# Attention products on four 64x64 TensorE tiles in a fused attention and feed-forward kernel

## The chip, the cores and the metric

One core of one Trainium2 chip. The metric is the device time of one execution in microseconds, the median of several runs. The profile is of one further execution, whose own time is given beside its span.

## What is computed

Eight batches of eight heads, 576 positions, head size 64, go through an attention whose softmaxes stand on the queries and keys alone, so that it is two small products per head. Its result, 4608 tokens of 512 features, goes through a two-layer network with a gated nonlinearity.

```python
q_s = softmax(q, axis=-1)                      # over the 64 features
k_s = softmax(k, axis=2)                       # over the 576 positions
kv  = einsum('bhsd,bhse->bhde', k_s, v)        # 64 x 64 per head
x   = einsum('bhsd,bhde->bhse', q_s, kv)       # then (batch, position) x (head, feature)
h   = x @ w_in                                 # 512 -> 2048
out = (h * sigmoid(beta * h)) @ w_out          # 2048 -> 512
```

## The kernel before

**Slabs.** The tokens are done in nine slabs of 512: slab t (0 to 7) is the first 512 positions of batch t, slab 8 the last 64 positions of all eight batches. Each slab has two halves of 64 full matmuls (128 rows, 128 columns, 512 moving columns, bf16). The first half (`pass1_tile`, L670; `pass1_mm`, L647) makes 16 tiles of 128 hidden features from four 128-feature parts of `XT`, rotating over the PSUM banks 0 to 2; ScalarE applies Silu with beta as scale (L655) into `GT`. The second half (`pass2_group`, L739) makes four groups u of 128 tokens over the 16 hidden tiles, in banks 3 and 4; VectorE copies the result out (L713) and SP stores it.

**Attention of one batch.** Heads are handled in four pairs hp. ScalarE takes exp of the queries (`exp_q`, L292) and keys (`exp_k`, L300). VectorE or GpSimd divides the queries by their sums (`norm_main`, L332) and a DMA transposes them into `QT` (`t_dma`, L454; batches 0 and 1 transpose on TensorE, `t_steps`, L376). The values are cast with a column of ones beside them (`cast_v`, L353). The keys' exps lie in `EK` as 128 columns per position group: for partitions 0 to 63 the first head's 64 features and zeros, for partitions 64 to 127 zeros and the second head's (a key tensor's partition holds nine consecutive positions of one head, 64 partitions per head). So one 128x128 matmul with 65 moving columns per group j (nine of them) accumulates the product of both heads of a pair and, in column 64, the keys' sums (`kv_steps`, L418). VectorE takes the reciprocal and scales the two 64x64 blocks into the diagonal of `KVD` (`kvd`, L403), whose other half is zero (`homes_vk`, L228). One 128x128 matmul per pair then gives the transposed output (`out_mm`, L438), which VectorE copies into `XT` (`out_step`, L443). The 64 remaining positions of two batches go together (`load_qrem`, L262; `exp_qr`, L327; `norm_rem`, L344; `tr_dma`, L462; `outr_steps`, L468), into `XT8` for slab 8. Batch 0's key-value product alone uses two 64x64 tiles (`kv_tiles`, L529), from keys' exps kept in `GT`.

**Order.** There are no queues of ready work: each engine runs its instructions in the order in which the program adds them, and `Program.plan` (L91) derives the semaphore waits from what each reads and writes. An instruction increments its engine's semaphore if any other one depends on it, also where only a later overwriting does. Matmuls of a slab are counted as slots 1 to 128 (`tick`, L785), 1 to 64 in the first half; a list `todo` gives the slot at which attention work is put between them. In slab t from 2 to 6 the attention of batch t+1 is done so (`attn`, L485): the 36 key-value matmuls one by one at slots 8 to 36, the four output matmuls at 84 to 108, for odd batches the remainder's eight at 104 to 120. Slab 1 does batch 2 (`attn_late`, L495, slots 103 to 124) and batch 1's remainder (101.5 to 103). In slab t ScalarE also takes the exps of batch t+2 after its Silus (L849 on): queries first, then the remainder's queries, then keys; then SP loads batch t+4.

**Loads.** SP issues one DMA each for a batch's queries, keys and values (`load`, L275), two for a pair of batches' remaining queries. Before the slabs stands a head (L604 to L643): weights are loaded and cast (`cast_win`, L579), batch 0's attention is done, and `warm` matmuls (L505) fill waits.

The softmax here doesn't subtract the row's maximum and nothing guards it: scores larger than these inputs give would overflow.

## Time and profile before

| what | value |
|---|---|
| time, median of 3 runs | 285.43 us (284.8 to 285.46) |
| the profiled execution's own time | 284.93 us |
| its span, first to last instruction | 283.1 us |
| TensorE matmuls busy | 277.9 us, 98%, 1608 matmuls |
| ScalarE busy | 177.6 us, 63% |
| VectorE busy | 117.0 us, 41% |
| GpSimd busy | 38.1 us, 13% |
| DMA, data queue of SP | 48.77 MB, 55.1% of the 16 engines' span |
| full matmuls of the two layers | 576 and 592 |
| key-value matmuls 128x128, 65 columns | 252 |
| output matmuls 128x128, 512 columns | 32 |

Matmuls are pipelined and the profile models their ends, so a matmul's mean duration (379 ns for 512 columns) is longer than the distance from one start to the next. What a matmul costs is read from starts: over a stretch, length by count. PE's busy share says that TensorE never lacks something to do, not that each thing is cheap. A line such as L373 is a helper through which all matmuls go, so groups are told apart by what they write and read. A bracket at a line's end is the idle time before it and what ended it.

### The profile page before, as it was taken

To read this page: it belongs to the slowest core of one execution; us is meant where nothing else is said; L and a number is where in the kernel's file an instruction comes from. 1 tells how busy PE (TensorE), PEld (TensorE's weight loads), DVE (VectorE), ACT (ScalarE), POOL (GpSimd) and SP (SyncE) were. 2 spreads that over 40 slices of the span, in tenths; PEclk is the share of its full clock that TensorE was granted. 3 is DMA by queue.
4 is the path that set the end of the run, shared out by engine and by line. 5 is a ranking of instruction groups with operands and counts; after the bars stand their busy time and mean duration, and the time that the engine had idled before them with its cause. 6 is when DMAs were issued, how large, how long until landed. Compare 5 with 4: busy or idle time off the path is not lost.

```text
span 283.1 us, 3950 instructions
## 1 busy us (share of the span) xinstructions
PE 277.9 (98%) x1608; PEld 136.3 (48%) x1608; DVE 117.0 (41%) x218; ACT 177.6 (63%) x243; POOL 38.1 (13%) x57
## 2 busy tenths in 40 slices
PE   7899999999999999999999999999999999999995
PEld 3545454445455445544554445444544444444443
DVE  4665786218781348124831473055705300110012
ACT  6767787989978926795579636892660076017500
POOL 6622041216121032100130000000000000000000
PEclk9999999999999999999999999999999999999999
DMA  7999999999998999217960033002700030012022
GB/s 249 371 390 400 391 371 307 361 341 248 330 329 248 358 360 296 39 34 251 374 104 1 2 148 74 2 1 98 141 4 0 9 141 0 0 54 96 0 74 74
DMA packets 41467, 50.07 MB, mean 177 GB/s; under 512 B 20325, under 2 KB 28773, under 8 KB 40297
## 3 DMA queue, kind: packets, MB, share of 16 engines
q1 hardware_dynamic: 40496, 48.77, 55.1%
q10 hardware_dynamic: 952, 1.06, 1.1%
q8 instruction: 12, 0.20, 0.3%
q14 instruction: 7, 0.05, 0.0%
HBM read 36.71 MB, written 9.44 MB: 163 GB/s over the span
## 4 chain that ended last, share of the span: by engine, by line
PE 98%; DVE 0%; ACT 0%; issue 0%
PE PS L373 97%; PE PS L371 1%; ACT XT L544 0%; DVE XT L219 0%; DVE KVD L411 0%; ACT VB L358 0%; DVE O2S L734 0%; DVE RC L520 0%
## 5 line engine op out<-in xcount | busy, mean ns | idle before, releaser
L655 ACT ACTIVATE GT<-PS,BETA 128x512 bf16<-128x512 f32 x144 | 96.7, 689 | 79.1 <-PE PS L373 79.1
L373 PE MATMUL PS<-WOUT,GT 128*128 128x512 bf16 (+2 forms) x592 | 132.8, 373 | 0.0
L373 PE MATMUL PS<-XT,WIN 128*128 128x512 bf16 x576 | 132.2, 379 | 0.0
L373 PEld LDWEIGHTS PS<-XT,WIN 128*128 128x128 bf16 x576 | 60.2, 106 | 59.2 <-ACT GT L655 0.4
L373 PEld LDWEIGHTS PS<-WOUT,GT 128*128 128x128 bf16 x592 | 55.4, 98 | 61.8
L713 DVE COPY O2S<-PS 128x512 f32<-128x512 f32 x33 | 22.7, 687 | 107.7 <-PE PS L373 107.7
L373 PE MATMUL PS<-VB,EK 128*128 128x65 bf16 x252 | 33.3, 193 | 0.0
L358 POOL CAST VB<-VF 128x576 bf16<-128x576 f32 (+1 forms) x29 | 21.1, 729 | 77.9 <-DMA VF<-in_v_dram 73.5
L309 ACT ACTIVATE EK<-KF 64x1152 bf16<-64x1152 f32 x24 | 27.8, 1157 | 0.4
L339 DVE TENSOR_REDUCE QS<-EQ 128x8 f32<-128x512 bf16 (+1 forms) x22 | 20.1, 913 | 15.4 <-ACT EQ L297 15.3
L373 PEld LDWEIGHTS PS<-VB,EK 128*128 128x128 bf16 x252 | 20.0, 98 | 6.5
L449 DVE CAST XT<-PS 128x512 bf16<-128x512 f32 x24 | 16.4, 690 | 10.9 <-PE PS L373 10.9
L297 ACT ACTIVATE EQ<-QF 128x512 bf16<-128x512 f32 x32 | 17.8, 619 | 2.0 <-DMA QF<-in_q_dram 1.8
L341 DVE TENSOR_TENSOR EQ<-EQ,QI 128x1024 bf16<-128x1024 bf16 (+1 forms) x14 | 15.9, 1132 | 0.5
L373 PE MATMUL PS<-QT,KVD 128*128 128x512 bf16 x32 | 12.2, 380 | 0.3 <-DVE KVD L411 0.3
L341 POOL TENSOR_TENSOR EQ<-EQ,QI 128x512 bf16<-128x512 bf16 x8 | 8.3, 1042 | 17.3 <-DVE QI L340 17.0
L373 PE MATMUL PS<-XT 128*128 128x512 f32 x10 | 7.7, 903 | 1.5 <-DVE XT L219 1.5
L411 DVE TENSOR_TENSOR KVD<-PS,RC 64x64 bf16<-64x64 f32 (+2 forms) x28 | 8.6, 308 | 0.9
L297 ACT ACT_TABLE_LOAD x6 | 7.7, 1283 | 0.1
L655 ACT ACT_TABLE_LOAD x5 | 6.4, 1283 | 0.1
L432 DVE RECIPROCAL RC<-PS 128x4 f32<-128x4 f32 (+2 forms) x9 | 1.6, 177 | 10.0 <-PE PS L373 9.9
L319 ACT ACTIVATE EK<-KF 64x576 bf16<-64x576 f32 (+1 forms) x6 | 5.0, 842 | 1.0 <-DMA KF<-in_k_dram 0.9
(54 smaller groups left out, 85.9 us busy)
## 6 DMA issues: line engine op xcount, KB each, us to landing
out_dram<-O2S SPq DMA_DIRECT2D x8, 1024.0 KB, 5.1
KF<-in_k_dram SPq DMA_DIRECT2D x6, 1152.0 KB, 8.4
VF<-in_v_dram SPq DMA_DIRECT2D x6, 1152.0 KB, 11.2
QF<-in_q_dram SPq DMA_DIRECT2D x6, 1024.0 KB, 7.6
KF<-in_k_dram SPq DMA_DIRECT2D x8, 288.0 KB, 8.3
VF<-in_v_dram SPq DMA_DIRECT2D x8, 288.0 KB, 8.6
WST<-in_moe_w_in_dram SPq DMA_DIRECT2D x8, 256.0 KB, 7.9
O2S<-in_moe_w_in_dram SPq DMA_DIRECT2D x4, 512.0 KB, 11.9
```

What stands on the lines that cost most here:

```text
L297: add(ACTE, lambda e, o=o, a=a: e.activation(o, a, ACT.Exp), r=[("qf", i, hp)], w=[("eq", i, hp)])
L309: add(ACTE, lambda e, o=o, a=a: e.activation(o, a, ACT.Exp), r=[("kf", i, h) for h in hps], w=[("ek", i, h, e_) for h in hps])
L319: add(ACTE, lambda e: e.activation(o, a, ACT.Exp), r=[("kf", i, h) for h in hps], w=[("ek", i, h, e_) for h in hps])
L339: add(DVE, lambda e: e.tensor_reduce(s_, a, AX.X, ALU.add), r=ks, w=[("qs", i, hp0)])
L341: add(eng, lambda e: e.tensor_tensor(a, a, vb, ALU.mult), r=ks + [("qi", i, hp0)], w=ks)
L358: add(eng, lambda e: (e.copy if eng == ACTE else e.tensor_copy)(o, a), r=[("vf", i, hp), ("vone", i)], w=[("vb", i, hp, h) for h in ((0, 1 ...
L371: add(PE, lambda e: e.transpose(o, l, r_), r=r, w=w, bank=[bk])
L373: add(PE, lambda e: e.matmul(o, l, r_, start=start, stop=stop, tile_position=tp), r=r, w=w, bank=[bk])
L411: add(DVE, lambda e, o=o, a=a, s_=s_: e.tensor_tensor(o, a, s_, ALU.mult), r=[("ps", bk)] + [("rc", i, h) for h in hps], w=[("kvd", i, h, ...
L449: add(eng, lambda e: (e.copy if eng == ACTE else e.tensor_copy)(XT[i][:, hp, :], PS[bk][:, :]), r=[("ps", bk)], w=[("xt", i, hp)], bank=[bk])
L655: add(ACTE, lambda e: e.activation(GT[:, f, :], PS[bk][:, :], ACT.Silu, scale=BETA[:, f:f + 1]), r=[("ps", bk), "beta"], w=[("gt", f)], ba ...
L713: add(eng, lambda e: (e.copy if eng == ACTE else e.tensor_copy)(O2S[t % 2][:, u, :], PS[bk][:, :]), r=[("ps", bk)], w=[("o2", t % 2, u)], ...
```

## The change

Batches 2 to 7 do both attention products on four 64x64 tiles of TensorE: tile (row, column) at (0,0), (64,64), (0,64), (64,0). The first two take the two heads of one pair, the other two those of the next pair, so that for pairs 1 and 3 the first head's product lands in the lower half of PSUM's partitions and the second's in the upper. For that the query load puts the heads of pairs 1 and 3 in swapped places, in four DMAs of two heads each in place of one (`load_swapped`), and the remainder's query load likewise in eight in place of two. Each output matmul swaps them back. `EK` now has 64 columns per group and no zeros for these batches, with one exp over all 128 partitions; `KVC` takes the place of `KVD` for them. `EKD`, with zeros, remains for batch 1.

All attention matmuls of a slab stand in one place: in slab t from 2 to 6 at slot 92, and the key-value product there is that of batch t+2, a slab earlier than before. In slab 1 the key-value product of batch 2 stands at slot 95 and a block at 113; the remainder of batch 1 at 94 to 95, on full matmuls as before. ScalarE takes the exps of the keys before those of the queries (batch 2 apart), and copies half of the outputs into `XT`.

```diff
+        SLOTS = ((0, 0, 1), (4, 4, 1), (2, 3, 4), (3, 2, 4))
+        def load_swapped(b):
+            i = b % 2
+            for x, (s0, d0, n) in enumerate(SLOTS):
+                a = bass.AP(qt_h, (b * H + s0) * S * D,
+                            [[4 * D, 128], [n * S * D, 2], [1, 4 * D]])
+                o = bass.AP(QF[i], d0 * 4 * D, [[H * 4 * D, 128], [n * 4 * D, 2], [1, 4 * D]])
+                add(SP, lambda e, o=o, a=a: e.dma_start(o, a),
...
+        def exp_kc(b, hp, n=1):
+            i = b % 2
+            o = bass.AP(EK[i], hp * KW, [[NHP * KW, 128], [1, n * KW]])
+            a = bass.AP(KF[i], hp * KW, [[NHP * KW, 128], [1, n * KW]])
...
+        def tile_mm(bk, ro, co, c, w, l, r_, start, stop, r):
+            mm(PS[bk][co:co + 64, c:c + w], l, r_, start, stop, r=r, w=[("ps", bk)], bk=bk,
+               tp=(ro, co))
+        def quad(hp):
+            return ((hp, 0, 0), (hp, 64, 64), (hp + 1, 0, 64), (hp + 1, 64, 0))
+        def kv_quads(b, bks):
+            i = b % 2
+            for a in (0, 2):
+                for j in range(NG):
+                    for hp, ro, co in quad(a):
+                        p = slice(ro, ro + 64)
+                        tile_mm(bks[hp % 2], ro, co, VW * (a // 2), D + 1, EK[i][p, hp, j, :],
+                                VB[i][p, hp, j, 0:D + 1], j == 0, j == NG - 1,
+                                [("ekc", i, hp), ("vb", i, hp, 0), ("vb", i, hp, 1), ("vone", i)])
+            for y in range(2):
...
+                add(DVE, lambda e, v_=v_, s_=s_: e.reciprocal(v_, s_), r=[("ps", bk)],
...
+                add(DVE, lambda e, o=o, p_=p_, vb=vb: e.tensor_tensor(o, p_, vb, ALU.mult),
...
+        def out_quads(b, bks):
+            i = b % 2
+            for a in (0, 2):
+                for hp, ro, co in quad(a):
+                    p = slice(ro, ro + 64)
+                    tile_mm(bks[hp], ro, co, 0, SM, KVC[i][p, hp, :], QT[i][p, hp, :], True, True,
+                            [("kvc", i, hp), ("qt", i, hp)])
             for hp in range(NHP):
+                eng, bk = (ACTE if hp % 2 else DVE), bks[hp]
...
+        def outr_quads(b, bks):
+            pi = b // 2
+            for a in (0, 2):
+                for e_ in range(2):
+                    for hp, ro, co in quad(a):
+                        p = slice(ro, ro + 64)
+                        tile_mm(bks[hp % 2], ro, co, 256 + (a // 2) * 128 + e_ * 64, 64,
+                                KVC[e_][p, hp, :], QTR[p, hp, 64 * e_:64 * e_ + 64], True, True,
+                                [("kvc", e_, hp), "qtr"])
...
+        def block(b):
+            out_quads(b, (5, 6, 7, 0))
+            if b % 2 and b > 1:
+                outr_quads(b, (1, 2))
+            if b + 1 < B:
+                kv_quads(b + 1, (1, 2))
...
-                todo = spread(outr_steps(1), 101.5, 103) + attn_late(2)
+                todo = spread(outr_steps(1), 94, 95)
+                todo += [(95, lambda: kv_quads(2, (1, 2))), (113, lambda: block(2))]
             elif t < 7:
-                todo = attn(t + 1)
+                todo = [(92, lambda: block(t + 1))]
```

The head is put in a new order. Batch 0's keys' exps lie in `EK[0]`; its last value cast is done whole by GpSimd (before, half by ScalarE), the cast of the weights' part 0, 3 by GpSimd in place of VectorE. Two long warm matmuls go and two short ones come; the second pair's transposes come before the first key-value product, the third output before the last product. The clearing of `EK[1]` in slab 0 goes.

```diff
         norm_main(0, 1, 1, POOL)
         go(t_steps(0, (0,), (3,)))
         turn_beta()
-        warm(1, 0, True)
         norm_main(0, 2, 1, POOL)
         norm_main(0, 3, 1, POOL)
+        go(t_steps(0, (1,), (4,)))
         kv_tiles(0, 7)
-        go(t_steps(0, (1,), (4,)))
-        warm(1, 0, True)
+        warm(1, 0)
         cast_v(0, 2)
-        cast_v(0, 3, POOL, 1)
-        cast_win(0, 1, POOL)
-        cast_win(0, 2, POOL)
+        cast_v(0, 3)
+        for m in range(1, NM):
+            cast_win(0, m, POOL)
         cast_win(1, 0, POOL)
         go(t_steps(0, (2,), (5,)))
+        warm(1, 0)
         kv_tiles(1, 1)
         out_now(0, 0, 0, ACTE)
         go(t_steps(0, (3,), (6,)))
         warm(1, 3)
+        kv_tiles(2, 7)
         out_now(0, 1, 5, ACTE)
-        kv_tiles(2, 7)
-        cast_v(0, 3, ACTE, 0)
         cast_win(0, 0, DVE)
         warm(1, 3)
+        out_now(0, 2, 0, ACTE)
         kv_tiles(3, 1)
-        out_now(0, 2, 0, ACTE)
```

## The prediction

> **What bounds the kernel now.** I read the page first. Its chain of work that ended last names one engine, and its slices show that engine full from the second slice on, while the DMA engines are full only for the first 16 slices (7.08 us each, so to about 113 us).

> ```profile
> PE   7899999999999999999999999999999999999995
> ...
> DMA  7999999999998999217960033002700030012022
> ...
> PE 98%; DVE 0%; ACT 0%; issue 0%
> ```

> So a TensorE nanosecond saved after some 113 us shortens the run; one saved earlier may only meet a transfer sooner. Next the busy time by stretch, one stretch per half slab (start and end, length, then busy time of PE, PEld, DVE, ACT, POOL). The slabs' starts come from the timeline of PE: slab 2 at 75.93, slab 7 at 224.69.

> ```profile
> 105.77:120.71 14.94, 14.94 (x102) 7.77 (x100) 7.03 (x10) 10.29 (x15) 3.30 (x4) 1.00 0.63 169
> 120.71:135.39 14.68, 14.68 (x70) 6.66 (x69) 4.74 (x7) 10.52 (x13) 0.00 (x0) 1.00 0.50 162
> 224.69:238.50 13.81, 13.81 (x66) 6.77 (x64) 0.69 (x1) 10.29 (x15) 0.00 (x0) 1.00 0.19 77
> 238.50:252.31 13.81, 13.81 (x65) 6.26 (x64) 2.08 (x3) 0.71 (x2) 0.00 (x0) 1.00 0.00 0
> ```

> Slab 7 has no attention: 13.81 us per half, 0.2158 us per matmul of 512 columns. Slab 3's first half, with 36 key-value matmuls, is 1.12 longer (31 ns each); its second, with four output matmuls, 0.86 longer (4 x 0.2158). Odd batches add 0.23 for eight remainder matmuls (14.91 in slabs 2, 4, 6). ACT is busy for 10.5 of 14.7 there, so it follows.

> Slabs 2 to 6 take 224.685 - 75.930 = 148.755; ten pure halves are 138.13. **The attention's whole price there is 10.62 us**; that is what can be won.

> **What the tiles cost in this trace.** The kernel already uses two tiles, in the head (batch 0). Timeline of PE (start, duration, line, count):

> ```profile
> 10.76 0.39 PE L371 MATMUL PS<-IDB,EQ 128*128 128x128 bf16 x4
> 11.08 0.47 PE L373 MATMUL PS<-VB,GT 64*64 64x65 bf16 x18
> 11.48 0.39 PE L373 MATMUL PS<-QT,KVD 128*128 128x512 bf16 x1
> ...
> 12.64 0.39 PE L373 MATMUL PS<-QT,KVD 128*128 128x512 bf16 x1 [0.33 <-DVE KVD L411]
> 12.96 0.47 PE L373 MATMUL PS<-VB,GT 64*64 64x65 bf16 x18
> 13.37 0.39 PE L373 MATMUL PS<-WARM 128*128 128x512 bf16 x1
> ```

> The 512-column matmul at 12.64 streams until 12.86; the next full one starts at 13.37. In between lie 0.51 us for 18 tile matmuls. Their single records show nine pairs, the second of a pair 3.5 ns after the first, pairs 32.4 ns apart: 0.29 us. The other **0.215 us is going into and out of the tiled mode** (0.10 and 0.11). A pair step of 32.4 ns equals the 31 to 32 ns of a full 65-column matmul[...].

> There is a second thing in the same place. VectorE waits for the last of those matmuls:

> ```profile
> 10.04 0.17 DVE L520 RECIPROCAL RC<-PS 128x1 f32<-128x1 f32 x1 [0.79 <-PE PS L371]
> ```

> The tile matmuls started between 9.205 and 9.489, yet the trace's semaphore records show PE's increments at 9.433, 9.467 and so on to 10.014: 34 ns apart. **Increments go one at a time, at 34 ns**, and the matmuls of a pair run ahead of them (16 ns each). At worst 15 were outstanding, and the stream did not slow.

> [...]

> **The change part by part.**

> *Key-value product, six batches.* Removed: 36 x 31.2 ns = 1.12 each. Added: 72 tile matmuls in 18 steps of four. At the pair's step this is 18 x 32.4 = 0.583. Bounds: 0.583 if four tiles go as fast as two; 1.17 if only two ever run together (36 steps); 2.45 (72 x 34 ns) if PE is held to the pace of its increments. I take 0.583: the pairs outran their increments, and a step didn't feel its instruction count.

> *Output, six batches.* 4 x 0.2158 = 0.863 becomes two steps of four, 0.432 (0.863 if in pairs). *Remainder, batches 3, 5, 7.* 0.234 becomes four steps, 0.130 (upper 0.54 by increments). *Mode changes.* One block costs 0.215; slab 1 has two.

> *Sum for slabs 2 to 6*, where a block holds output(t+1), the odd batch's remainder and key-value(t+2): slabs 2 and 4: 0.432 + 0.130 + 0.583 + 0.215 = 1.36; slabs 3 and 5: 1.23; slab 6 has no next batch: 0.78. Together 5.96 against 10.62: **4.66 us saved**, all on PE's chain.

> *Slab 1.* Before, its second half has 16.05 - 13.81 = 2.23 of attention. After: remainder of batch 1 unchanged 0.234, key-value(2) with its mode changes 0.80, then a block of 1.23: 2.26. No gain, and a new wait: the whole of output(2) now stands at slot 113, some 71.5 us, and the kernel goes no further until the transposed queries of pairs 2 and 3 are there. They are issued last behind batch 3's load:

> ```profile
> 66.01 3.76 SPq L459 DMA_TRANSPOSE QT<-EQ  x2
> ```

> They land at 70.48 and 71.69; before, pair 2 was wanted only at 73.3. From 71.69: 0.22 + 0.58 + 0.11 + 15 x 0.2158 = 4.15, so slab 2 can't start before 75.85 (75.93 now). Queued behind that wait on PE is everything; the DMA order that causes it is not changed, and the engines are full until there.

> *Head.* V's last cast goes from ScalarE (13.55 to 14.01) wholly to POOL, one weight cast from DVE to POOL, the transposes come before the product, two long warm matmuls go. The waits [0.40 <- ACT VB] and for the first weight cast shrink: landed at 13.09 it can be cast right after the third product's scaling, near 13.1 to 13.5, so the first layer starts near 13.65 in place of 14.99. The cover is thin: weights for columns 1024 on land at 20.39 and are wanted at 20.8, and in slab 0's second half batch 1's normalisation and the output weights are held by DMA. Timeline of DVE:

> ```profile
> 37.94 1.24 DVE L341 TENSOR_TENSOR EQ<-EQ,QI 128x512 bf16<-128x512 bf16 x1
> 39.10 2.08 DVE L569 TENSOR_SCALAR WOUT<-O2S,RB 128x512 bf16<-128x512 f32 x4
> ```

> The first of these scales is ready at 39.5; PE uses it at 40.28. So of 1.34 us at most 0.76 passes here, and the wait at 71.69 eats that. Head and slab 1 together: 0.0 to 0.8 saved, I take 0.1.

> *Covered work.* ScalarE: key exps go from four of 1157 ns to two (same columns, all partitions), 2.3 us less per slab; it takes two of the four XT copies (0.58 each) after its exps, which end about 7.3 us after a first half, where the copies come at 5.8; the next slab needs them only at 13.8. DVE: two copies of 0.69 less, four short scalings in place of three operations. POOL: casts unchanged; the second memset of slab 0 goes. SP: three more issues per query load, six more per remainder pair, at 0.43 to 0.5 us each, same packets; at most 4.5 us in a queue that otherwise waits for stores (111.9 us in the SP waits). Keys and values of batch 4 on are wanted 10 us earlier; the nearest, V(4), lands at 83.0 and is cast by 86.3, against some 96. All at nothing; if batch 3's cast (from 68.8) were late by 1 us, slab 1 pays 1 us.

> **The sum.** The profiled execution is 284.93, span 283.13 and 1.80 around it. 284.93 - 4.66 - 0.1 = 280.2; the same taken off the median 285.43 is 280.7. I say **280.5**.

> **Rivals.** (1) *Slower: the increments hold PE.* Nearly every tile matmul increments, because a later batch overwrites what it read. Batches 6 and 7 have no successor and escape. If few more than 15 can be outstanding, the products of batches 2 to 5 cost 2.45 each, 1.87 over; two fall into slab 1 (3.74, less 0.7 from the head), two into slabs 2 and 3 (3.74), the remainders of 3 and 5 add 0.41 each: -4.66 + 3.05 + 3.74 + 0.83 = +2.96, 288. It decides for slower above about 25 ns per tile matmul. For: 55 would be outstanding. Against: 15 left no mark. (2) *Only two tiles run at once*, so the change doesn't do what it says: +0.432 per output, +0.583 per product, +0.13 per remainder, 4.88 in slabs 2 to 6 and 1.6 - 0.7 in slab 1: +1.1, 286. For: the trace has only tiles that differ in rows and columns both. (3) *Only the products run at half pace*[...]: -4.66 + 2.72 + 0.47 = -1.5, 283.5. (4) *Head gain survives*: 279.6.

> **Chances.** Forecast 0.57, (1) 0.12, (2) 0.07, (3) 0.18, (4) 0.06. The range 279.2 to 285.5 takes in (3) and (4) and the bounds between; it leaves out (1) and (2), 0.19. About 0.3% (0.86 us) is what can be told from no change: faster means below 284.6. Forecast, (4) and most of (3) give 0.78 faster; 0.06 within; 0.16 slower.

> **What would show it.** Right: first halves of slabs 2 to 6 at 13.81, second halves near 15.1, slab 2's start near 75.9 with a short PE wait for the transposes before it; a product's 72 matmuls inside 0.6 us, VectorE's reciprocals some 2.5 us after the first of them. Wrong: tile matmuls 16 ns apart (rival 2 or 3) or 34 (rival 1), PE idle at slot 92 on key, value or query data, or the first layer not near 13.7.

## The result and the profile after

| what | before | after |
|---|---|---|
| time, median, side by side | 285.12 us (284.79 to 285.46) | 288.95 us (288.75 to 289.84) |
| ratio, 95% interval | | 1.014, 1.0114 to 1.0167 |
| the profiled execution's own time | 284.93 us | 288.75 us |
| its span | 283.13 us | 286.96 us |

The kernel is slower by 1.4%, where 280.5 was forecast. The page of after, its slices (7.17 us each), its chain of work that ended last, and the row of the tile matmuls of the key-value product:

```profile
PE   7899999999999799999999799999999999999995
...
DMA  7999999999999998607970006000640030002023
...
PE 75%; DMA 14%; SPq 5%; DVE 4%; issue 1%
...
L390 PE MATMUL PS<-VB,EK 64*64 64x65 bf16 x504 | 11.2, 191 | 3.3 <-DVE XT L556 3.0
```

Two slices of TensorE now stand at 7 that stood at 9: the 14th (93.3 to 100.4 us) and the 23rd (157.8 to 165.0). The chain is no longer TensorE from end to end. It runs back through VectorE, and through a DMA and SP's queue from there. The row names the releaser: VectorE's copy into `XT` at L556, the copy of the *remainder*. Next the half slabs of slabs 2 and 3, in the columns that the prediction used:

```profile
78.00:91.80 13.80, 13.75 (x65) 6.75 (x65) 7.66 (x10) 10.10 (x15) 3.01 (x4) 1.00 1.16 278
91.80:109.90 18.10, 16.29 (x160) 8.34 (x161) 4.76 (x11) 8.84 (x12) 2.68 (x4) 1.00 1.08 347
109.90:123.70 13.80, 13.75 (x64) 6.75 (x64) 6.29 (x7) 10.07 (x15) 4.21 (x4) 1.00 0.56 138
123.70:139.90 16.20, 15.99 (x144) 8.20 (x145) 4.10 (x9) 9.26 (x13) 0.00 (x0) 1.00 0.57 190
```

First halves are down to the 13.81 us of a half without attention. Second halves stand far above the forecast of 15.17 and 15.04, and the first of them has 1.8 us in which TensorE does nothing. Lengths of all halves, from one half's first weight load to the next one's (the after trace lacks 28 of 1168 full matmuls' own records, and has all of their weight loads; differences are taken before rounding):

| slab | before, whole slab | after, whole slab | difference | forecast |
|---|---|---|---|---|
| start of slab 1 | 44.91 | 44.41 | -0.50 | -0.1 with slab 1 |
| 1 | 14.76 + 16.05 | 14.76 + 18.79 | +2.75 | (row above) |
| 2 | 14.94 + 14.91 | 13.81 + 18.11 | +2.08 | -0.86 |
| 3 | 14.93 + 14.68 | 13.81 + 16.17 | +0.38 | -0.75 |
| 4 | 14.94 + 14.91 | 13.81 + 17.18 | +1.15 | -0.86 |
| 5 | 14.93 + 14.68 | 13.81 + 15.17 | -0.62 | -0.75 |
| 6 | 14.94 + 14.91 | 13.81 + 14.60 | -1.43 | -1.44 |

The differences make +3.80 of the span's +3.83. Slab 6, the one block without a product, came out as forecast; slab 5, whose product is batch 7's, nearly. Everything that failed lies in the products of batches 2 to 5, in the two blocks with a remainder ahead of a product, and in slab 1.

**A block with a remainder.** Timeline of TensorE in slab 2 (start, duration, line, operation, count, idle before):

```profile
98.13 0.63 PE L390 MATMUL PS<-QT,KVC 64*64 64x512 bf16 x8
98.59 0.29 PE L390 MATMUL PS<-QTR,KVC 64*64 64x64 bf16 x16
100.37 2.02 PE L390 MATMUL PS<-VB,EK 64*64 64x65 bf16 x72 [1.49 <-DVE XT L556]
102.55 1.24 PE L390 MATMUL PS<-WOUT,GT 128*128 128x512 bf16 x5 [0.16 <-issue]
```

The outputs take 0.46 from their start to the remainder's, as forecast (0.432). The remainder's 16 matmuls start within 0.10 us. Then TensorE waits, and the timeline of VectorE shows for what:

```profile
98.60 1.29 DVE L540 CAST XT<-PS 128x512 bf16<-128x512 f32 x2 [2.19 <-PE PS L390]
99.81 0.75 DVE L556 CAST XT<-PS 128x256 bf16<-128x256 f32 x2
103.21 0.17 DVE L525 RECIPROCAL RC<-PS 128x2 f32<-128x2 f32 x1 [2.66 <-PE PS L390]
```

The diff's `block` gives banks 1 and 2 to `outr_quads` and the same two to `kv_quads`. The product can't overwrite the remainder there until VectorE has copied it out, and those copies stand behind two output copies of 0.65 each. By the single records the wait is 1.65 for bank 1 and, two matmuls later, 0.33 more for bank 2: **1.98 us, in slabs 2 and 4**.

**A product without that wait.** Starts of every fourth tile matmul of two products, in ns from the first; batch 3's stands in slab 1, batch 7's in slab 5:

```
matmul     1   5   9  13  17  21  25  29   33   37   41   45   49    53    57    61    65    69    72
batch 3    0  29  64  97 129 158 193 225  349  487  623  759  896  1033  1169  1306  1443  1579  1682
batch 7    0  29  64  97 129 158 192 225  271  382  411  448  480   516   548   581   611   645   673
```

They agree within a ns up to the 29th matmul, fours about 32 ns apart: four tiles do run at once. From the 31st on batch 3's starts are 34 ns apart one by one (some 136 per four), the pace of PE's increments, whose records in this product are 34 ns apart as well. Its 72 matmuls all increment, since batch 5 overwrites what they read; batch 7 has no successor, and only two of its 72 do. From first to last start: 1.60, 1.68, 1.84 (with the 0.33 in it) and 1.68 for batches 2 to 5, against 18 steps in the forecast, of which the last start comes after some 0.56. Less the 0.33 that is the bank's, **that is 1.04 + 1.12 + 0.95 + 1.12 = 4.23 us.**

**Slab 1.** TensorE there, and SP's issues ahead of it:

```profile
66.41 1.79 PE L390 MATMUL PS<-VB,EK 64*64 64x65 bf16 x72
68.35 3.83 PE L390 MATMUL PS<-WOUT,GT 128*128 128x512 bf16 x17 [0.16 <-issue]
72.42 0.88 PE L390 MATMUL PS<-QT,KVC 64*64 64x512 bf16 x8 [0.23 <-DMA QT<-EQ]
73.13 1.87 PE L390 MATMUL PS<-VB,EK 64*64 64x65 bf16 x72
```

```profile
57.13 6.89 SPq L277 DMA_DIRECT2D QRF<-in_q_dram  x8
65.52 4.59 SPq L476 DMA_TRANSPOSE QT<-EQ  x2
```

The first transpose is issued no later than before (66.01) and the second 0.34 later (68.86 for 68.52), but they land at 72.38 and 72.85 in place of 70.48 and 71.69. The outputs wait for both, 0.30 and 0.23: **0.53 us**.

**The account.** Forecast for slabs 2 to 6, -4.66; for slab 1, +0.03; start of slab 1, -0.50 measured. With increments 4.23, banks 3.96, transposes 0.53 and 0.12 that batch 7's product takes over the forecast, the sum is +3.71, against +3.80 in the table.

### The profile page after: what moved, and what is told of

Same layout as the page of the kernel before. It is cut to its first block, busy times and chain, and to the rows that moved or that the text cites. A ratio compares the mean times of both kernels' runs of the same rounds, so it can differ in the third digit from the quotient of the medians.

```text
span 287.0 us, 4482 instructions
## 1 busy us (share of the span) xinstructions
PE 275.3 (96%) x1841; PEld 136.8 (48%) x1870; DVE 105.7 (37%) x211; ACT 168.8 (59%) x242; POOL 37.7 (13%) x56
## 3 DMA queue, kind: packets, MB, share of 16 engines
q1 hardware_dynamic: 41072, 48.77, 56.3%
## 4 chain that ended last, share of the span: by engine, by line
PE 75%; DMA 14%; SPq 5%; DVE 4%; issue 1%
PE PS L390 75%; DMA VF<-in_v_dram 5%; DMA O2S<-in_moe_w_in_dram 4%; DMA O2S<-in_moe_w_out_dram 4%; SPq L261 2%; SPq L639 1%; DMA QT<-EQ 1%; SPq L294 1%; DVE XT L540 1%; DVE QS L356 1%; DVE WOUT L632 1%; SPq L481 0%; SPq L251 0%; PE PS L388 0%; DVE WIN L643 0%
## 5 line engine op out<-in xcount | busy, mean ns | idle before, releaser
L390 PE MATMUL PS<-WOUT,GT 128*128 128x512 bf16 (+2 forms) x574 | 125.2, 373 | 1.7 <-issue 1.1
L390 PE MATMUL PS<-XT,WIN 128*128 128x512 bf16 x566 | 125.9, 379 | 0.5
L375 POOL CAST VB<-VF 128x576 bf16<-128x576 f32 x29 | 22.4, 773 | 79.3 <-DMA VF<-in_v_dram 57.4
L339 ACT ACTIVATE EK<-KF 128x1152 bf16<-128x1152 f32 (+1 forms) x16 | 15.9, 1035 | 1.1 <-DMA KF<-in_k_dram 0.8
L390 PE MATMUL PS<-VB,EK 64*64 64x65 bf16 x504 | 11.2, 191 | 3.3 <-DVE XT L556 3.0
L390 PEld LDWEIGHTS PS<-VB,EK 64*64 64x64 bf16 x504 | 10.3, 105 | 5.1 <-issue 3.8
L540 DVE CAST XT<-PS 128x512 bf16<-128x512 f32 x12 | 7.7, 686 | 11.1 <-PE PS L390 11.1
L540 ACT CAST XT<-PS 128x512 bf16<-128x512 f32 x12 | 6.4, 583 | 6.2 <-PE PS L390 6.1
L332 ACT ACTIVATE EKD<-KF 64x576 bf16<-64x576 f32 (+1 forms) x6 | 5.0, 842 | 1.1 <-DMA KF<-in_k_dram 0.9
L357 DVE RECIPROCAL QI<-QS 128x8 f32<-128x8 f32 (+1 forms) x22 | 5.0, 226 | 0.8
```

The costliest lines, as they stand in the source:

```text
L332: add(ACTE, lambda e: e.activation(o, a, ACT.Exp), r=[("kf", i, h) for h in hps], w=[("ek", i, h, e_) for h in hps])
L339: add(ACTE, lambda e: e.activation(o, a, ACT.Exp), r=[("kf", i, h) for h in range(hp, hp + n)], w=[("ekc", i, h) for h in range(hp, hp + n)])
L357: add(DVE, lambda e: e.reciprocal(v_, s_), r=[("qs", i, hp0)], w=[("qi", i, hp0)])
L375: add(eng, lambda e: (e.copy if eng == ACTE else e.tensor_copy)(o, a), r=[("vf", i, hp), ("vone", i)], w=[("vb", i, hp, h) for h in ((0, 1 ...
L390: add(PE, lambda e: e.matmul(o, l, r_, start=start, stop=stop, tile_position=tp), r=r, w=w, bank=[bk])
L540: add(eng, lambda e, eng=eng, bk=bk, hp=hp: (e.copy if eng == ACTE else e.tensor_copy)(XT[i][:, hp, :], PS[bk][:, :]), r=[("ps", bk)], w=[ ...
```

## The experiments

The theory is that the forecast lacked three waits: the increments of a burst (with some 30 outstanding, that is, of matmuls that have started and not recorded yet, the next ones go at 34 ns), the banks, the transposes. The rivals: the tiles themselves slow down after some 30, whatever increments; VectorE as such is late, wherever the remainder stands; the eight small loads of the remainder's queries make the transposes late; the head gained something that slab 1 gave back, or gained nothing.

Second halves of slabs 1 to 6 in the profiled executions, and the sum of slabs 2 to 6:

| kernel | s1 | s2 | s3 | s4 | s5 | s6 | slabs 2 to 6 |
|---|---|---|---|---|---|---|---|
| before | 16.05 | 14.91 | 14.68 | 14.91 | 14.68 | 14.91 | 148.76 |
| after | 18.79 | 18.11 | 16.17 | 17.18 | 15.17 | 14.60 | 150.30 |
| e1_last_readers | 19.99 | 17.28 | 15.27 | 17.19 | 15.17 | 14.60 | 148.57 |
| e2_remainder_early | 19.22 | 16.53 | 16.17 | 15.58 | 15.17 | 14.83 | 147.35 |
| e3_both | 17.40 | 15.62 | 15.27 | 15.58 | 15.17 | 14.83 | 145.54 |
| e4_all_increment | 18.47 | 18.11 | 16.18 | 18.11 | 16.17 | 14.60 | 152.23 |
| e10_product_in_halves | 18.25 | 15.89 | 15.54 | 15.74 | 15.33 | 14.83 | 146.40 |
| e9_remainder_after_transposes | 16.42 | 15.62 | 15.27 | 15.57 | 15.17 | 14.83 | 145.54 |

**e1: fewer increments.** Of a product's matmuls only those of the last position group count as readers, so that 8 of 72 increment; the work is the same.

```diff
         for k in r:
             deps.extend(self.writer.get(k, ()))
-            self.readers.setdefault(k, []).append(op)
+            if last:
+                self.readers.setdefault(k, []).append(op)
...
-                                [("ekc", i, hp), ("vb", i, hp, 0), ("vb", i, hp, 1), ("vone", i)])
+                                [("ekc", i, hp), ("vb", i, hp, 0), ("vb", i, hp, 1), ("vone", i)],
+                                last=j == NG - 1)
```

> The tile matmuls of the key-value product increment PE's semaphore only for the last position group of each head (8 of 72 in place of all 72 for batches 2 to 5); instructions, order and data are the same. Theory I (PE may run some 32 increments ahead and then goes at their pace, 34 ns each): the products of batches 2 to 5 fall from 1.6 to 1.8 us to about 0.58, as batch 6's already is; two of the four savings (0.93 and 1.12) count fully in slabs 2 and 3, of the two in slab 1 only the second (1.12), since the first ends in the wait for the transposed queries. Together 3.2: near 285.8. Rival J (34 ns is what PE's sequencer needs for a tile's weight load and matmul once its queue has run dry): no change, 289. Rival of the write-up's prediction that only two tiles run at once: no change either.

Measured: 287.79 us (before, beside it, 284.84), ratio 1.0087, 1.0060 to 1.0115. The products of batches 2 to 5 start within 0.67, 0.75, 0.98 (bank 2 waited for in it) and 0.75 us. Slabs 2 and 3 give 0.83 and 0.90, so the increments were what held them. But slab 1 became longer, 19.99. Timeline of its TensorE, a window over it (PE, PEld, DVE, ACT, POOL busy, clock), and the page's clock row:

```profile
72.90 0.89 PE L391 MATMUL PS<-QT,KVC 64*64 64x512 bf16 x8 [1.55 <-DMA QT<-EQ]
73.62 0.96 PE L391 MATMUL PS<-VB,EK 64*64 64x65 bf16 x72
74.52 5.10 PE L391 MATMUL PS<-WOUT,GT 128*128 128x512 bf16 x15
```

```profile
74.50:78.20 3.70, 3.70 (x17) 1.33 (x11) 0.99 (x5) 1.30 (x2) 0.00 (x0) 0.54 0.93 315
```

```profile
PEclk9999999999799999999999999999999999999999
```

Batch 2's product is over sooner, so TensorE comes 0.8 us earlier to transposes that land no earlier (72.86), and waits 1.55 us. From 74.69 on, 1.8 us after that wait, the granted clock was 0.5 for 3.41 us, full matmuls 0.43 apart in place of 0.2158, which costs 1.71. What two products had won there was given back. The six runs lie at 286.1 to 286.2 (two) and 287.7 to 288.3 (four). The two have a mean granted clock of 1.0, the four of 0.987 to 0.994, and one stretch of 3.41 us at half clock makes 0.994. So the clock fell somewhere in the four and not in the two; that it fell in slab 1 is seen in the profiled one alone. Without a fall the edit comes to 286.15, near the 285.8 expected.

**e4: more increments.** The other direction: every tile matmul increments, those of batches 6 and 7 too.

```diff
+        op.inc = inc
...
-                    r=r, w=w, bank=[bk])
+                    r=r, w=w, bank=[bk], inc=tp is not None)
```

> The suspected cost is added where it was missing: every tile matmul increments, so the products of batches 6 and 7 too (72 each in place of 2) and the remainder of batch 7 (16). Nothing else differs. Theory I: batch 6's product goes from 0.58 to about 1.5, batch 7's from 0.67 to 1.68, each on PE's chain: +1.9 to +2.1, near 291. Rival J and the two-tile rival: no change, 289.

Measured: 291.65, ratio 1.0239, 1.0206 to 1.0273. Timeline of TensorE, batch 7's product:

```profile
192.77 1.87 PE L391 MATMUL PS<-VB,EK 64*64 64x65 bf16 x72
194.57 0.60 PE L391 MATMUL PS<-WOUT,GT 128*128 128x512 bf16 x2
```

Batch 7's product goes from 0.67 to 1.682 us between first and last start, the number of batch 3's in the kernel after; batch 6's from 0.905 to 1.834. Slabs 4 and 5 grow by 0.93 and 1.00 and now equal slabs 2 and 3; no other slab from 2 to 6 moves. So it isn't the place, the batch, the banks or the tiles.

**e2: the remainder in a place of its own**, at slot 84, eight full matmuls ahead of the block, with the same banks; increments as they were.

```diff
         def block(b):
             out_quads(b, (5, 6, 7, 0))
-            if b % 2 and b > 1:
-                outr_quads(b, (1, 2))
...
                 todo = [(92, lambda: block(t + 1))]
+                if t % 2 == 0:
+                    todo.append((84, lambda: outr_quads(t + 1, (1, 2))))
```

> The remainder's tile matmuls of batches 3, 5 and 7 stand at slot 84, in a tiled stretch of their own, and no more between the outputs and the key-value product at slot 92. Theory W (in slabs 2 and 4 the product waits 1.65 us, and 0.33 once more, for VectorE's copies of the remainder out of banks 1 and 2, which stand behind two output copies): 3.96 goes, three mode changes of 0.215 come, net 3.3: near 285.6. Rival (VectorE or a later wait is the limit there, and the wait only moves): within 0.5 of 289.

Measured: 286.71, ratio 1.0057, 1.0040 to 1.0074. Timeline of TensorE in slab 2, where the product no longer waits:

```profile
97.41 0.32 PE L390 MATMUL PS<-QTR,KVC 64*64 64x64 bf16 x16
97.66 1.90 PE L390 MATMUL PS<-WOUT,GT 128*128 128x512 bf16 x8
99.49 0.63 PE L390 MATMUL PS<-QT,KVC 64*64 64x512 bf16 x8
99.95 1.87 PE L390 MATMUL PS<-VB,EK 64*64 64x65 bf16 x72
```

Slabs 2 and 4 give 1.58 and 1.61, the wait of 1.98 less a further change of mode (0.215 by the prediction) and what else the own place costs; slab 6, which had no wait, pays 0.23 for it. VectorE's work is the same, and it makes nobody wait once the remainder stands eight matmuls earlier: the place was the cause, not the engine (other banks in the old place weren't tried). The time expected was 285.6. In the profile 0.35 of the difference lies in slabs 2 to 6 (2.95 saved, 3.3 expected), 0.43 in slab 1 (19.22), where the transposes made it wait 0.70 and 0.25, and 0.61 in slab 0's second half (16.70 for 16.09 in the kernel after), which the edit doesn't touch and which was 16.09 again in e3.

**e3: both edits.**

> Both edits of the two runs before this. If the two costs are separate (theories I and W both hold) the savings add, 3.2 + 3.3: near 282.5, faster than the kernel before by 2.6. If they cover one another (the wait gives the increments time to drain, so that removing one lets the other show), less than the sum by up to 1 us: 283.5. If slab 1's wait for the transposes takes part of it, more than 283.5.

Measured: 283.58 (283.47 to 283.74), ratio 0.9952, 0.9937 to 0.9967: faster than before. Slabs 2 to 6 lie 4.77 under those of after; e1 alone gave 1.73 there and e2 alone 2.95, together 4.68. In these slabs the two waits add up and share next to nothing. The time is the third case of the expectation: slab 1 still waits for the transposes, 0.70 and 0.26.

**e10: the limit shown without removing an increment.** e2 with all increments, but each product cut into two bursts of 36 (pairs 0 and 1, then 2 and 3), six full matmuls apart. It adds a tiled stretch, with its two changes of mode, for each product.

```diff
-        def kv_quads(b, bks):
+        def kv_quads(b, bks, half):
...
-            for a in (0, 2):
+            for a in (half,):
...
                 todo = [(92, lambda: block(t + 1))]
+                if t < 6:
+                    todo.append((98, lambda: kv_quads(t + 2, (1, 2), 2)))
```

> On top of e2_remainder_early, with all its increments: each key-value product of 72 tile matmuls is cut into two bursts of 36, six full matmuls (1.3 us) apart (batch 2: slots 95 and 101; batch 3: 113 and 119; later ones 92 and 98). Theory I, with some 32 outstanding before PE is held: each burst runs its first 32 freely and drains before the next; a product of batches 2 to 5 costs two times about 0.3 to 0.45 in place of 1.68, and one mode change of 0.215 more: 0.6 to 0.8 saved each on batches 3, 4, 5, lost 0.2 each on 6 and 7: 1.4 to 2.0 faster than e2_remainder_early, near 285.0. Rival (every increment costs PE 34 ns less the pace, whenever it comes): 36 at a time as dear as 72, plus 6 mode changes: 1.2 slower than e2, 287.9.

Measured: 284.54, ratio 0.9992, 0.9983 to 1.0000, and 2.2 us less than e2. In the profiles 0.95 of that lies in slabs 2 to 6: slabs 2 and 3 give 0.64 each, slabs 4 and 5, whose products hardly increment, pay 0.16 each for the cut. Slab 1 gives 0.97; the rest is slab 0's second half, which was long in e2. Timeline of TensorE in slab 2:

```profile
98.07 0.63 PE L390 MATMUL PS<-QT,KVC 64*64 64x512 bf16 x8
98.53 0.64 PE L390 MATMUL PS<-VB,EK 64*64 64x65 bf16 x36
99.32 1.24 PE L390 MATMUL PS<-WOUT,GT 128*128 128x512 bf16 x5 [0.16 <-ACT XT L542]
100.50 0.56 PE L390 MATMUL PS<-VB,EK 64*64 64x65 bf16 x36
100.98 0.39 PE L390 MATMUL PS<-WOUT,GT 128*128 128x512 bf16 x1
```

As many increments in all, but in two parts: 36 at 34 ns take 1.22 us, and the bursts' starts lie 1.97 us apart, so that by this estimate the first 36 are recorded before the second burst begins. The second burst's starts span 0.370, with the first 34 at full pace and the last two 34 ns apart; the first, directly behind the eight outputs, spans 0.452, with 34 ns from the 31st on. Half as many at once cost far less than half, because the first 30 to 34 of each burst went at full pace.

What is outstanding can be counted in the traces of e2 and e4, which have every matmul's record: matmuls that increment and have started, less the increments recorded so far. In each of the ten products whose matmuls all increment, the count rises to 31 and stays there while the matmuls go at 34 ns, whether 30 or 34 started freely; so it does in batch 4's product in the trace of after. In e3, with few increments, it stays at 6 or less.

**e8: does a full matmul feel its increments?** The edit of e1 in the kernel *before*, whose key-value matmuls stand one by one between full ones. PE's semaphore records fall from 1299 to 1155, by 144 and not by the 180 of the expectation.

> The kernel before, with its key-value matmuls of batches 2 to 7 (and two pairs of batch 1) incrementing only for the last position group of a pair. Theory I: full matmuls stand one by one between matmuls of 216 ns, so increments never run 30 behind: no change, within 0.3. Rival (each increment costs TensorE time wherever it is): 180 increments go, several us faster.

Measured: 285.03 (14 runs) against 284.97 (28 runs), ratio 1.0004, 0.9995 to 1.0013. No: here, with full matmuls of 216 ns between them, 144 increments fewer change nothing that shows. With e1, e4 and e10: in these runs increments cost where they came faster than one in 34 ns for so long that 31 were outstanding.

**e7: the head alone.** The new head order in the kernel before, and nothing else.

> The kernel before with the new order of the head alone (casts, transposes, warm matmuls). The prediction gave the head 0 to 0.8, with DMA in slab 0 taking back the rest of 1.34. In the changed kernel's trace slab 1 starts 0.5 sooner than before. In the kernel before nothing waits for the transposes in slab 1, so what passes slab 0 should reach the end: 0.3 to 0.5 faster, near 284.4. Rival (slab 0's second half waits for the loads in any case): 284.8, no change.

Measured: 285.16 (13 runs) against 284.97, ratio 1.0004, 0.9996 to 1.0013. The first layer starts 0.90 earlier (14.08 for 14.98), slab 1 0.54 earlier (44.37 for 44.91), slab 2 no earlier (75.78 for 75.72, both by weight loads). Timeline of TensorE in slab 1:

```profile
71.67 0.39 PE L373 MATMUL PS<-QT,KVD 128*128 128x512 bf16 x1 [0.44 <-DMA QT<-EQ]
```

An output waits for the transposes, which land at 71.62 and 72.35 here (70.48 and 71.69 in before): the head's gain ends there, also without any other part of the change, and the 0.3 to 0.5 expected don't arrive.

**e5, e6, e9: why the transposes are late.** e5 is e3 with the remainder's queries loaded by two DMAs of 128 KB, as before, the heads exchanged in three exps in place of by the load.

```diff
-                for x, (s0, d0, n) in enumerate(SLOTS):
...
+                a = bass.AP(qt_h, (b + h) * H * S * D + SM * D, [[D, SR], [S * D, H], [1, D]])
...
+            for d0, s0, n in ((0, 0, 2), (2, 3, 1), (3, 2, 1)):
+                o = bass.AP(EQR[i], d0 * D, [[H * D, 128], [4 * D, 2], [1, n * D]])
```

> On top of e3_both: the remaining queries are loaded in two DMAs of 128 KB as in the kernel before, in place of eight of 32 KB, and the exchange of heads is done by the exp that reads them (three instructions in place of one). Theory D (the eight small loads delay what is queued behind them; in e3_both the last lands at 72.46 and the two transposes at 72.66 and 73.16, against 69.37, 70.48 and 71.69 before): the transposes land near 70.5 and 71.7 again, output(2) no longer waits (0.70 and 0.26 in e3_both): near 282.6. Rival (bytes alone set the landing): no change, 283.6.

Measured: 283.16 (283.07 to 284.84), ratio 0.9944, 0.9924 to 0.9963, not to be told from e3's 0.9952. The remainder landed at 69.38 (72.46 in e3), the transposes still at 71.94 and 72.71, and 1.10 and 0.53 of waiting were left. That the eight small loads are the cause is not confirmed.

The traces say more. Batch 3's values, loaded just ahead of the remainder, land at 68.7 to 69.9 in all but e9. Counted from there, the second transpose lands 2.91 us later in before, 3.10 in e8 and 3.15 in e7, but 3.93 to 4.13 later in after, e1 to e6 and e10, with eight loads as with two. So about 1 us of it goes neither with these loads nor with the head, but with some other part of the change; the four query loads per batch are one, and no run takes them away.

e6 is e5 with slab 1's block five slots later, 118 for 113:

> On top of e5_remainder_two_loads: the block of slab 1 stands at slot 118 in place of 113. If theory D holds and the wait is gone already, no more than 0.2 comes of it, near 282.5; if the transposes still land late, up to 0.9 comes of it, near 282.7.

Measured: 282.68, ratio 0.9910, 0.9892 to 0.9929. It still waits 0.42 and 0.62, as the transposes now land at 72.73 and 73.59. e9 is e6 with the remainder's load for batches 2 and 3 issued behind the transposes, and its exp at slab 1's end:

```diff
-            if b % 2:
+            if b % 2 and b != 3:
                 load_qrem(b - 1)
...
+                    load_qrem(2)
...
+            if t == 1:
+                exp_qr(1)
```

> On top of e6_and_block2_at_118: the remaining queries of batches 2 and 3 are loaded after batch 2's transposes in SP's queue in place of before, and their exp moves behind slab 1's output copies. In e6 the transposes land at 72.73 and 73.59, 2.5 and 3.4 after that load, and output(2) waits 0.42 and 0.62. If their place in the queue sets that, they land some 0.7 sooner or more and most of the 1.0 goes: near 281.8. Rival (the transposes are slow by themselves, in whatever place): under 0.3, 282.5.

Measured: 281.72 (281.39 to 282.32) against 284.83, **ratio 0.9884, 0.9869 to 0.9899: faster than both kernels**. The transposes land at 71.43 and 72.39, and the output waits for nothing; slab 1's second half is 16.42 (17.48 in e6; the intervals of the two times just overlap). Timeline of TensorE, slab 1 and slab 2:

```profile
72.90 0.63 PE L388 MATMUL PS<-QT,KVC 64*64 64x512 bf16 x8
73.35 0.96 PE L388 MATMUL PS<-VB,EK 64*64 64x65 bf16 x72
...
96.72 0.63 PE L388 MATMUL PS<-QT,KVC 64*64 64x512 bf16 x8
97.18 0.96 PE L388 MATMUL PS<-VB,EK 64*64 64x65 bf16 x72
```

So the remainder's load ahead of the transposes was part of it: behind them in SP's queue, it lets them land 1.30 and 1.20 sooner than in e6, by one profile each. What else makes them late stays open.

## Why the prediction was wrong

**The step that failed most: the key-value product.** "I take 0.583: the pairs outran their increments, and a step didn't feel its instruction count." The second half is right (fours 32 ns apart, as pairs were); the first was drawn from 15 outstanding increments, and the burst has 72. The trace of before could not show where the stream is held, and the upper bound of that very step, 2.45, stood among the rivals and had no part in the sum. Measured: 1.60 to 1.84 where all increment, 0.67 to 0.75 where few do; 4.23 us in four products. In the trace of before the increments, 34 ns apart, only made VectorE wait for the last matmul (0.79 us ahead of 10.04). Here, with 31 outstanding, the matmuls themselves went at 34 ns each.

**Rival 1 had the mechanism, and its size was off.** "If few more than 15 can be outstanding, the products of batches 2 to 5 cost 2.45 each." Some 30 go free first, so the price is about 1.05 each and not 1.87, and the remainders' 16 matmuls pay nothing (0.10 us from first to last). That batches 6 and 7 escape was right, and e4 shows why. With only this rival's true price the sum would have been 280.2 + 4.2 = 284.4: no slowdown. That the rival's total, 288, lies so near the measured 288.95 is luck: it had 8.3 us of increments, where 4.23 were measured, and the banks' 3.96, which it didn't have, filled the gap.

**The term that was missing: the banks.** The sum wrote "output(t+1), the odd batch's remainder and key-value(t+2)" as durations in a row, and no line of it asks whose banks they write. The two calls with (1, 2) stand next to each other in the diff. 3.96 us, as much as the increments; neither sum nor rival had it, and together with the increments it turns the sign. The kernel after shows what two such calls in a row cost (1.98 us each time), and e2 that the wait goes when they stand apart.

**Costed at nothing: a later landing of the transposes.** The place was named: "the kernel goes no further until the transposed queries of pairs 2 and 3 are there." But their landing was kept at 71.69, from before, and it came at 72.85. The first of the two transposes carries pairs 0 and 1, not 2, and was late as well: 72.38 for 70.48, where the first output stood at 71.61 in before. In after the two waits are 0.53; in e1 and e2, where they land later still (e1: 72.86, e2: 73.36) or TensorE arrives sooner, the first alone is 1.55 and 0.70. "Same packets" was true of the bytes (48.77 MB) and not of the packets: the queue had 41072 in place of 40496, and the remainder's eight issues took SP 6.89 us where two took 4.50. That these are the cause isn't shown (e5, e7); by e9 a different order of that queue removes the wait.

**The head.** The first layer was to start at 13.65 and started at 14.20. That "at most 0.76 passes here, and the wait at 71.69 eats that" holds: 0.50 passed, and e7 has none of it left at slab 2.

**What was right.** Both changes of mode at 0.215 and the remainder at 0.130 (slab 6: 13.81 + 0.432 + 0.130 + 0.215 = 14.59, measured 14.60); outputs 0.46; four tiles at once (fours 32 ns apart), which was the author's estimate and not shown by the trace of before, against rivals 2 and 3; first halves 13.81; ScalarE, GpSimd and the earlier keys and values at nothing, as nothing in slabs 2 to 6 waits for them. e3 and e9 come to -3.22 in slabs 2 to 6, against -4.66: three remainders in their own place cost 0.23 more each (0.69), and the rest is in the four products, 0.13 to 0.23 longer each than forecast (slab 5: 15.17 for 15.04; slab 3: 15.27 for 15.04).

**What stays open.** Why a product with few increments takes 0.67 to 0.75 and not 0.56: in batch 7's of after, and batch 5's of e1, the 33rd to 36th matmul start 8 ns apart and a gap of 86 ns follows; this wasn't tried. What besides the remainder's place in SP's queue makes the transposes late. Why the clock fell in e1.

## What to carry to other kernels

Before pricing a burst of small matmuls, count how many of them increment a semaphore: here TensorE ran until 31 increments were outstanding and then went at 34 ns each, so let only the last reader of a buffer count. List the PSUM bank of every group that is put directly behind another one, with who empties it and what that engine does first (here 1.98 us a time). When work is gathered in one place, take all its inputs' landing times anew, because what was late and hidden for one part of it can now be waited for by the whole (0.53 us in slab 1 of the kernel after).
